# Four edits in a gated mix of a state-space layer and a long convolution: where two steps stand in the head, who scales two tiles, the order of two loads, and how the last tile is finished

## The chip, the cores and the metric

The kernel runs on one core of a Trainium2 chip. A core has five engines that run side by side, each in the order of its own instructions: TensorE (PE in the profile; its weight loads are PEld), VectorE (DVE), ScalarE (ACT), GpSimd (POOL) and SyncE (SP). SP issues loads and stores, POOL issues the transfers that add to their destination. The metric is the time of one execution on the device in microseconds (us).

## The reference, cut to what matters

Two branches of a sequence of 2048 positions with 1024 channels are mixed by a gate that is worked out from x.

```python
g = _sigmoid((x * gate_w).sum(-1, keepdims=True))
a = _A_ref(x, ...)      # a diagonal complex state per p:  h[t] = Lam_bar * h[t-1] + B_bar x[t]
                        # y = 2 Re(h C^T) + x * Dskip
b = _B_ref(x, k, v, ...)  # k: 4 taps per channel; kv = taps(k) * v
                        # y = causal convolution of kv with ssm_k (length 2048), plus kv * ssm_D;  b = x * y
return g * a + (1 - g) * b
```

## The kernel before, in words

**Branch B** (the convolution) runs first, channel block by channel block (eight blocks of 128 channels, index `c`). Taps, foldings and a transform by tables of sines and cosines are matmuls (`taps`, `fold_K`, `fwd_K`, `fwd_V`); the products of the two spectra are made on VectorE (`products`), the way back is matmuls again (`inverse`, tables `CI` and `SI`), and the result goes to a scratch in DRAM (`cv_scr`). ScalarE moves most PSUM tiles to SBUF.

**Branch A** (the state) works on four blocks of 512 positions (`tb`) and four groups of two state tiles (`g`). `Bu` multiplies x by B on TensorE; ScalarE copies the result out of PSUM; `turn_U` scales it on ScalarE into tiles named `Q`, which POOL adds to `U` by transfer; `scan` rotates, runs the recurrence on VectorE and rotates back into `hb`, then makes the odd positions into `U`. `Cy` and `Cy_g` multiply `hb` and `U` by C for each of the 16 output tiles of 128 positions. Every tile of C (eight, `CT[0]` to `CT[7]`) must first be turned (`turn_C`): ScalarE makes a scaled copy `m` of the other half (imaginary against real), the half itself is scaled in place, and the two are added, by POOL's transfer (`by_sum`, tiles 0, 1, 4 and 5) or by VectorE.

**The order** is written out by hand. `put` (line 94 is the line that nearly all instructions show) chains every instruction of an engine behind the one before it, so the order of the Python calls is the order on each engine. Many helpers are generators, and `step` and `run` place their pieces. `filler` (line 1361) takes one piece at a time from the list `on_act` between the pieces of `Bu`.

The places of the four edits:

- The head, lines 1076 to 1120. `angles` is `inverse_angles`, the reduced angles of the inverse table on VectorE; `turns` is `inverse_table` (its Abs, then sine `SI`, then cosine `CI`, all on ScalarE); `sp` is `state_params`, whose second step makes `abv`, the rate `rv` (an exponential on ScalarE) and two more small columns; its third step writes `abv` again, so it waits for `rv`.
- `turn_C`, lines 1274 to 1292, and the main loop over 16 scans, lines 1433 to 1480. Tiles 4 and 5 lend their `m` from the four buffers `Q` that `turn_U` uses too.
- The loads on SP around line 1241: C's tiles 0, 1 and 2, with B's third block `BT[2]` in between; then, at line 1295, B's fourth block `BT[3]` and C's tile 3.
- The last block of four output tiles, lines 1482 to 1500. The four PSUM tiles (two banks each: two halves of 512 channels) take groups 0 to 2 of all four tiles, then group 3 tile by tile. `finish` multiplies the B part by x beforehand, then takes a tile out of PSUM, on VectorE (tiles 0, 2 and 3 of the block) or by ScalarE and one addition (tile 1), and stores it; tile 3 is finished in two halves, and its matmuls of the last tile are sorted so that the first half is done first.

PSUM has room for four such tiles, which are taken in turn; a fifth waits until the first has been read.

Of the kernel before, what the change touches and what calls it, by code (L numbers as in the profile page):

```python
# [9 lines left out]
ALU = mybir.AluOpType  # L10
# [10 lines left out]
def kernel(  # L21
# [37 lines left out]
    NT = S // 128  # L59
# [45 lines left out]
    def tt(o, a, b, op):  # L105
        put("dve", V.tensor_tensor, out=o, in0=a, in1=b, op=op)
# [863 lines left out]
    def rows_of(ap, t_):  # L970
        t0 = t_ // 4 * TB + t_ % 4 // 2 + t_ % 2 * HB
        return ap[t0:t0 + HB - 1:2, :]
# [34 lines left out]
        act(gd, rows_, func=ACT.Identity, scale=gcols[:, t_:t_ + 1])  # L1007
        gather(pbb, gd)

    def Cy_g(tb, tl, ps, g, last):  # L1010
        X = hbs[tb, g] if tl < 2 else Us[tb, g][1]
        tsl = slice(tl % 2 * 128, tl % 2 * 128 + 128)
        steps_ = [(j, c, dh) for j in range(2) for c in range(2) for dh in range(2)]
        if tb * 4 + tl == NT - 1:
            steps_.sort(key=lambda s_: s_[2])
        for j, c, dh in steps_:
            mm(ps[dh], X[:, c, j, tsl], CT[2 * g + j][:, c, dh * 512:(dh + 1) * 512],
               g == 0 and j == 0 and c == 0, last and j == 1 and c == 1)

# [13 lines left out]
    def product(t_):  # L1033
        pbb, xr = ios[t_]
        tt(xr, xr, pbb, ALU.mult)
# [3 lines left out]

    def store(t_):  # L1040
        move(rows_of(of, t_), gas.pop(t_))

    def finish(t_, ps=None):

        rows = rows_of(of, t_)
        product(t_)
        xr = ios.pop(t_)[1]
        if ps is None:
            yield
            ga = gas.pop(t_)  # L1050
            tt(ga, ga, xr, ALU.add)
        else:
            yield
            ga = a_room(t_)
            for o, i in ps:
                put("dve", V.scalar_tensor_tensor, out=ga[:, o], in0=i, scalar=gcols[:, t_:t_ + 1], in1=xr[:, o],
                    op0=ALU.mult, op1=ALU.add)
                if len(ps) > 1:
                    move(rows[:, o], ga[:, o])
            if len(ps) > 1:  # L1060
                return
        move(rows, ga)


    def step(gen):
        next(gen, None)
# [31 lines left out]
    step(sp)  # L1098
    run(first)
    dg1 = dgs(1, True)  # L1100
    run(angles)
    load("kT", 1)
    load("v", 1)
    load("kn", 1)
    fwd_K(0, (0, 1))
    fwd_V(0, (0, 1))
    step(sp)
    step(turns)
    taps(1, dg1)
    step(sp)  # L1110
    step(turns)
    p0 = products(0, 0)
    steps(p0, 3)
    tv = times_v(1)
# [17 lines left out]
    for c in range(NC - 1):  # L1132
        n, nn = c + 1, c + 2
        if c == 0:
            load("kn", 2)
            load("kT", 2)
            load("v", 2)
            load_BT(0, 0)
            load_xT(0, (0,))
            p1 = products(0, 1)  # L1140
            fwd_K(n, (0, 1))
            step(p0)
            run(tv)
            dg = dgs(nn, True)
            steps(p1, 2)
            step(p0)
            step(p1)
            run(p0)
            taps(nn, dg)
            step(sp)  # L1150
            fwd_K(n, (2, 3))
            step(p1)
            step(sp)
            fwd_V(n)
            run(p1)
            run(fold_K(nn))
            tv = times_v(nn)
            step(tv)
            load("kn", 3)
            load("kT", 3)  # L1160
            load_BT(0, 1)
            apart = spread(3)
            step(apart)
            load_xT(0, (1,))
            run(apart)
            lam_diag(0, lam_pool, True)
            continue
        if c == 6:
            put("pool", nc.gpsimd.tensor_copy, stamp, xTs[2][:, 0, 0:HB + 1:HB])
        tabs, back, prod = turn_table(c - 1) if c <= NG else none, inverse(c - 1), products(c)  # L1170
        step(old)
        step(tabs)
        if c == 6:
            step(parts)
        step(back)
        step(tv)
        steps(prod, 3)
        run(tv)
        step(old)
        step(tabs)  # L1180
        run(back)
        run(old)
        fk = none
        if nn < NC:
            dg = dgs(nn)
            if by_channel(nn):
                fk = fold_columns(nn)
                step(fk)
        if c == 2:
            step(parts)  # L1190
        fwd_K(n, (0, 1))
        if c in (2, 6):
            step(parts)
        fwd_K(n, (2, 3))
        if c == 4:
            step(parts)
        if c == 6:
            run(sp)
            s5p["Q"] = s5p["wu"]
            run(turns_U[2])  # L1200
            gate(0)
        step(prod)
        if nn < NC:
            if not by_channel(nn):
                fk = mirror_K(nn)
            step(fk)
            if c < 5:
                step(fk)
            if c == 4:
                step(parts)  # L1210
            if c == 1:
                load_BT(1, 0, True)
            elif c < 5:
                load("v", nn, True)
            step(parts)
            taps(nn, dg)
            if c == 5:
                load("v", nn)
                load_xT(2, held=True)
            if nn + 1 < NC:  # L1220
                load("kT", nn + 1, True)
                load("kn", nn + 1)
                apart = spread(nn + 1)
                step(apart)
                if c == 1:
                    load_BT(1, 1)
                elif c in (2, 3):
                    load_xT(1, (3 - c,))
                run(apart)
        step(prod)  # L1230
        run(fk)
        if n == NC - 1:
            overlap_K(n)
        run(prod)
        if nn < NC:
            tv = times_v(nn)
            step(tv)
            step(parts)
        else:
            run(next(tiles))  # L1240
            for pi in range(3):
                CT[pi] = ld.tile([128, 2, D], BF16, name="CTa", tag="ld")
                if pi == 0:
                    hold(CT[0][:, 0, 0:1])
                load_CT(pi)
                if pi == 0:
                    load_BT(2, 0)
                    load_BT(2, 1)
            run(next(tiles))
            run(next(tiles))  # L1250
        fwd_V(n, (0, 1))
        if c < 6 and c != 4:
            step(parts)
            if c in (1, 3):
                step(parts)
        fwd_V(n, (2, 3))
        if c in (4, 5):
            step(parts)
        if c == 1:
            lam_diag(1, lam_pool)  # L1260
        old = tabs
# [12 lines left out]
    def turn_C(pi):  # L1274
        by_sum = pi in (0, 1, 4, 5)
        if pi in (4, 5):
            m = [s5p["Q"].tile([128, D], BF16, name="Q") for c in range(2)]
        else:
            whole_m = m_pool.tile([128, 2, D], BF16, name="m")
            m = [whole_m[:, c] for c in range(2)]  # L1280
        for c in range(2):
            act(m[c], CT[pi][:, 1 - c], func=ACT.Identity, scale=mc2i[:, pi:pi + 1])
            yield
        for c, f in enumerate((c2r, mc2r)):
            if pi < 2:
                act(CT[pi][:, c], CT[pi][:, c], func=ACT.Identity, scale=f[:, pi:pi + 1])
            else:
                ts(CT[pi][:, c], CT[pi][:, c], f[:, pi:pi + 1], None, ALU.mult)
            if by_sum:
                gather(CT[pi][:, c], m[c])  # L1290
        if not by_sum:
            tt(CT[pi], CT[pi], whole_m, ALU.add)

    turning = [turn_C(pi) for pi in range(NP)]
    load_BT(3, 0)
    load_BT(3, 1)
    load_CT(3)
    with tc.tile_pool(name="fin", bufs=1, side="right") as fin:

# [133 lines left out]
    for j in range(NS):  # L1433
# [6 lines left out]
        advance(j)  # L1440
        for t in turning[2 * j:2 * j + 2]:
            run(t)
        on_act += [lambda t=t: step(t) for t in turning[2 * j + 2:2 * j + 4] for _ in range(2)]
        turn = turns_U[turned[j]] if j in turned else none
        if j != 10 and plan[j][0:1] != "G":
            step(turn)
# [34 lines left out]

    tb = NTB - 1
    t0 = tb * 4
    pss = []
    for tl in range(4):
        ps = ps2([128, 2, 512], "psy")
        halves = [(slice(h * 512, h * 512 + 512), ps[:, h]) for h in range(2)]
        pss.append(([ps[:, 0], ps[:, 1]], halves if tl == 3 else [(slice(0, D), flat(ps))]))
    for g in range(NG - 1):
        for tl in range(4):  # L1490
            Cy_g(tb, tl, pss[tl][0], g, False)
    fins = []
    for tl in range(4):
        fins.append(finish(t0 + tl, None if tl == 1 else pss[tl][1]))
        step(fins[tl])
    for tl in range(4):
        Cy_g(tb, tl, pss[tl][0], NG - 1, True)
        if tl == 1:
            scale_a(t0 + tl, pss[tl][1])
        run(fins[tl])  # L1500
# [1 line left out]
_INS = ['A_x', 'A_Lambda_re', 'A_Lambda_im', 'A_B_re', 'A_B_im', 'A_C_re', 'A_C_im', 'A_log_dt', 'A_Dskip', 'B_q', 'B_k', 'B_v', 'B_shift_k', 'B_ssm_k', 'B_ssm_D', 'gate_w']  # L1502
_OUTS = [((1, 2048, 1024), 'bfloat16')]
# [25 lines left out]
```

## Time and profile before

| | us |
|---|---|
| median of 3 runs | 384.97 (384.64 to 386.58) |
| the profiled execution, its own time | 384.57 |
| its span, first to last instruction | 382.8 |
| TensorE busy | 371.3 |
| VectorE busy | 371.2 |
| ScalarE busy | 303.6 |
| GpSimd busy | 81.8 |
| granted TensorE clock | 0.998 |

A row of the timeline holds start, length, engine, line, operation, what is written and read, the shapes, the count of merged instructions, and in brackets the idle time of the engine before it and what ended it. A row with a count merges neighbours of one kind; its length runs to the last one's end. A row of the chain holds start, length and what the chain went through. A weight load stands in front of every matmul, on its own track, while the matmul before it runs. About one matmul record in fifty is missing.

### The profile page before, as it was taken

The page shows a single profiled execution, that of the slowest core. Times are in us where ns is not written, and L with a number is a line of the kernel's source. Part 1 is how long each engine was busy: PE and PEld are TensorE (multiplying, and loading weights), DVE is VectorE, ACT ScalarE, POOL GpSimd, SP SyncE. Part 2 cuts the span into 40 slices and gives each one's busy share as a digit, 9 for nine tenths or more (in the row PEclk, how much of TensorE's full clock was granted, in tenths as well). Part 3 has the DMA queues.
Part 4 walks back from the last instruction along what each step waited for, and adds up shares of the span by engine and source line. Part 5 has one row for each costly group of instructions (what it writes and reads, how often), then busy time and mean ns, then how long its engine had stood idle before and what let it go on. Part 6 is the DMA issues. An engine that isn't in the chain of part 4 may idle for free.

```text
span 382.8 us, 6633 instructions
## 1 busy us (share of the span) xinstructions
PE 371.3 (97%) x2419; PEld 198.3 (52%) x2453; DVE 371.2 (97%) x599; ACT 303.6 (79%) x469; POOL 81.8 (21%) x108
## 2 busy tenths in 40 slices
PE   7899999999999999999999999989999999999995
PEld 5566458575584846744454444434444444444442
DVE  7999999999999999999999999999999999999996
ACT  5898998988979999786979699675989759937601
POOL 4011030020301102031003110413414323634100
PEclk9999999999999999999999999999999999999999
DMA  7979999998999997959999999986899999898903
GB/s 166 165 108 223 218 205 205 245 203 211 201 164 211 208 213 169 198 125 154 192 221 164 226 203 250 213 153 125 150 222 192 208 245 246 136 250 156 238 8 110
DMA packets 126402, 71.77 MB, mean 187 GB/s; under 512 B 104665, under 2 KB 107489, under 8 KB 126370
## 3 DMA queue, kind: packets, MB, share of 16 engines
q1 hardware_dynamic: 111232, 45.64, 55.4%
q0 software_dynamic: 12976, 25.17, 38.9%
q10 hardware_dynamic: 2162, 0.54, 0.8%
q8 instruction: 19, 0.31, 0.3%
q14 instruction: 13, 0.11, 0.1%
HBM read 15.48 MB, written 8.39 MB: 62 GB/s over the span
## 4 chain that ended last, share of the span: by engine, by line
PE 52%; DVE 30%; issue 9%; DMA 4%; ACT 3%; ACTq 1%; POOL 0%; DVEq 0%; POOLq 0%
PE psy L94 29%; PE both L94 15%; DVE BT L94 11%; DVE wkh L94 8%; DVE G L94 5%; DVE t L94 3%; PE psz L94 2%; DVE ks L94 2%; PE psk L94 2%; DMA CT<-Q 2%; DMA pbb<-cv_scr 1%; PE psv L94 1%; DMA rows<-in_gate_w_dram 1%; PE p L94 1%; PE taps L94 1%
## 5 line engine op out<-in xcount | busy, mean ns | idle before, releaser
L94 PEld LDWEIGHTS <-BT 128*128 128x128 bf16 x640 | 62.0, 98 | 48.3 <-issue 0.2
L94 PE MATMUL both<-xT,BT 128*128 128x512 bf16 x375 | 83.0, 379 | 0.4
L94 POOL DMA_DIRECT2D U<-Q x26 | 26.7, 1039 | 88.8 <-ACT Q L94 31.0
L94 PEld LDWEIGHTS <-hb 128*128 128x128 bf16 x256 | 24.9, 98 | 31.4 <-issue 1.6
L94 PEld LDWEIGHTS <-U 128*128 128x128 bf16 x240 | 23.5, 98 | 28.3
L94 PE MATMUL psy<-CT,hb 128*128 128x512 bf16 x157 | 36.3, 379 | 0.1
L94 ACT ACTIVATE Vh<-psv 128x1024 bf16<-128x1024 f32 x32 | 30.7, 1034 | 5.3 <-PE psv L94 5.3
L94 PE MATMUL psy<-CT,U 128*128 128x512 bf16 x149 | 34.6, 379 | 0.2
L94 ACT ACTIVATE Q<-U,lam 128x512 bf16<-128x512 bf16 (+1 forms) x52 | 29.9, 612 | 4.9 <-DMA CT<-Q 4.9
L94 DVE TENSOR_TENSOR_SCAN W<-rv,init,A 128x256 bf16<-128x256 f32 x48 | 32.2, 730 | 0.0
L94 POOL DMA_DIRECT2D G<-wkh x8 | 9.7, 1218 | 102.8 <-DVE wkh L94 102.8
L94 ACT ACTIVATE U<-both 128x512 bf16<-128x512 f32 x44 | 24.1, 595 | 8.0 <-PE both L94 7.5
L94 PEld LDWEIGHTS <-SF 128*128 128x128 bf16 x184 | 18.0, 98 | 19.7 <-issue 1.4
L94 PE MATMUL psk<-eok,SF 128*128 128x512 bf16 (+1 forms) x119 | 27.9, 354 | 0.3
L94 PE MATMUL psz<-G,CI 128*128 128x512 bf16 x64 | 24.3, 379 | 0.1
L94 PE MATMUL psz<-G,SI 128*128 128x512 bf16 x64 | 24.3, 379 | 0.0
L94 PE MATMUL psy<-CTa,hb 128*128 128x512 bf16 x94 | 22.6, 379 | 1.2 <-ACT U L94 1.0
L94 PE MATMUL taps<-dg,kT 128*128 128x128 bf16 (+1 forms) x352 | 21.7, 210 | 0.8 <-DMA kT<-in_B_k_dram 0.8
L94 PEld LDWEIGHTS <-kT 128*128 128x128 bf16 x352 | 21.0, 100 | 2.5 <-DMA kT<-in_B_k_dram 2.1
L94 DVE TENSOR_TENSOR wkh<-BT,Vh 128x3072 bf16<-128x3072 bf16 (+4 forms) x20 | 21.8, 1110 | 0.0
L94 DVE TENSOR_TENSOR wkh<-Kh,Vh 128x3072 bf16<-128x3072 bf16 (+2 forms) x16 | 21.2, 1348 | 0.0
L94 PE MATMUL psy<-CTa,U 128*128 128x512 bf16 x87 | 20.4, 379 | 0.1
(227 smaller groups left out, 846.1 us busy)
## 6 DMA issues: line engine op xcount, KB each, us to landing
U<-Q POOLq DMA_DIRECT2D x26, 256.0 KB, 5.3
G<-wkh POOLq DMA_DIRECT2D x6, 768.0 KB, 8.8
cv_scr<-cv SPq DMA_DIRECT2D x16, 256.0 KB, 5.7
kn<-in_B_ssm_k_dram SPq DMA_DIRECT2D x5, 512.0 KB, 4.0
v<-in_B_v_dram SPq DMA_DIRECT2D x5, 512.0 KB, 6.2
out_dram<-m SPq DMA_DIRECT2D x8, 256.0 KB, 4.5
BT<-cv_scr SPq DMA_DIRECT2D x7, 256.0 KB, 5.9
out_dram<-BT SPq DMA_DIRECT2D x7, 256.0 KB, 2.0
```

The lines of the kernel that those rows point to most:

```text
L94: i = f(*a, **kw)
```

## The change

1. **Head.** The second step of `state_params` moves up from behind the transforms, to stand between the first and the second tile of `fwd_K` and ahead of the angles; the step of the inverse table that makes the sine moves behind the second half of the first block's spectra, next to the cosine.
2. **C's tiles 4 and 5.** Their scaling in place moves from VectorE to ScalarE (`by_sum` instead of `pi < 2`), as two more pieces of their generators; the list of pieces for ScalarE no longer takes those of tiles 2 and 3, and takes four instead of two of tiles 4 and 5. So tile 4 is turned whole among the pieces of `Bu` 9, and tile 5 among those of `Bu` 10.
3. **Loads.** C's tile 2 is allocated and loaded after `BT[3]`, ahead of C's tile 3.
4. **The last tile.** Its second half gets a PSUM tile of its own, `rest`, and all its 16 matmuls (four groups) come after everything else. Its first half is taken out by ScalarE and one addition (`scaled_added`), the second by VectorE (`added`); the products stand directly ahead of each tile's end instead of all in front.

```diff
-    run(angles)
     load("kT", 1)
     load("v", 1)
     load("kn", 1)
-    fwd_K(0, (0, 1))
+    fwd_K(0, (0,))
+    step(sp)
+    run(angles)
+    fwd_K(0, (1,))
     fwd_V(0, (0, 1))
-    step(sp)
     step(turns)
     taps(1, dg1)
     step(sp)
-    step(turns)
     p0 = products(0, 0)
...
-            for pi in range(3):
+            for pi in range(2):
                 CT[pi] = ld.tile([128, 2, D], BF16, name="CTa", tag="ld")
...
         for c, f in enumerate((c2r, mc2r)):
-            if pi < 2:
+            if by_sum:
                 act(CT[pi][:, c], CT[pi][:, c], func=ACT.Identity, scale=f[:, pi:pi + 1])
             else:
                 ts(CT[pi][:, c], CT[pi][:, c], f[:, pi:pi + 1], None, ALU.mult)
             if by_sum:
                 gather(CT[pi][:, c], m[c])
+                yield
...
     load_BT(3, 0)
     load_BT(3, 1)
+    CT[2] = ld.tile([128, 2, D], BF16, name="CTa", tag="ld")
+    load_CT(2)
     load_CT(3)
...
-        on_act += [lambda t=t: step(t) for t in turning[2 * j + 2:2 * j + 4] for _ in range(2)]
+        if j > 0:
+            on_act += [lambda t=t: step(t) for t in turning[2 * j + 2:2 * j + 4] for _ in range(4 if j == 1 else 2)]
...
+    def added(t_, o, ps):
+        put("dve", V.scalar_tensor_tensor, out=a_room(t_)[:, o], in0=ps, scalar=gcols[:, t_:t_ + 1],
+            in1=ios[t_][1][:, o], op0=ALU.mult, op1=ALU.add)
+        move(rows_of(of, t_)[:, o], a_room(t_)[:, o])
+
+    def scaled_added(t_, o, ps):
+        ga, xr = a_room(t_), ios[t_][1]
+        act(ga[:, o], ps, func=ACT.Identity, scale=gcols[:, t_:t_ + 1])
+        tt(ga[:, o], ga[:, o], xr[:, o], ALU.add)
+        move(rows_of(of, t_)[:, o], ga[:, o])
+
+    pss = [ps2([128, 2, 512], "psy") for tl in range(4)]
+    banks = [[ps[:, 0], ps[:, 1]] for ps in pss]
     for g in range(NG - 1):
         for tl in range(4):
-            Cy_g(tb, tl, pss[tl][0], g, False)
...
+            Cy_g(tb, tl, banks[tl], g, False, (0, 1) if tl < 3 else (0,))
     for tl in range(4):
...
+        Cy_g(tb, tl, banks[tl], NG - 1, True, (0, 1) if tl < 3 else (0,))
+        product(t0 + tl)
+        if tl < 3:
+            (scaled_added if tl == 1 else added)(t0 + tl, slice(0, D), flat(pss[tl]))
+        else:
+            scaled_added(t0 + tl, slice(0, 512), banks[tl][0])
+    rest = ps2([128, 2, 512], "psy")[:, 0]
+    for g in range(NG):
+        Cy_g(tb, 3, [None, rest], g, g == NG - 1, (1,))
+    added(t0 + 3, slice(512, D), rest)
```

`Cy_g` has one more argument, the halves that it multiplies, and the sorting for the last tile is gone. The matmuls are the same 2453 in number.

## The prediction

> **What bounds the kernel now.** I read the page's first part, then the chain in order of time, then the busy times by stretch, then the timelines of the four places that the diff touches.
>
> ```profile
> span 382.8 us, 6633 instructions
> PE 371.3 (97%) x2419; PEld 198.3 (52%) x2453; DVE 371.2 (97%) x599; ACT 303.6 (79%) x469; POOL 81.8 (21%) x108
> ```
>
> ```profile
> 164.30 0.39 PE mirror L94
> ...
> 253.15 9.01 PE psy L94 x41
> ...
> 374.96 3.63 PE psy L94 x16
> ```
>
> ```profile
> 32.00:164.00 132.00, 130.46 (x1107) 82.86 (x1116) 131.41 (x126) 117.06 (x181) 16.63 (x21) 1.00 1.05 206
> 164.00:251.00 87.00, 86.20 (x477) 40.50 (x487) 86.10 (x135) 72.08 (x120) 19.13 (x21) 1.00 1.02 196
> 253.00:378.00 125.00, 124.22 (x595) 56.96 (x607) 122.92 (x274) 87.56 (x135) 39.26 (x46) 1.00 0.85 174
> ```
>
> The columns behind the length are busy PE, PEld, DVE, ACT, POOL, then the granted clock and the DMA share. Two engines are full at once: from 32 to 378 us neither TensorE nor VectorE idles by as much as 2% of a stretch. The chain runs over VectorE before 164, over TensorE after it. So an edit is worth time only if it takes work or a wait from both, or leaves the one that it doesn't help in no one's way. No edit changes TensorE's work; it can gain waits alone, and VectorE gains what is taken from it.
>
> **Head.** VectorE, then ScalarE, then TensorE:
>
> ```profile
> 19.86 0.18 DVE L94 TENSOR_TENSOR abv<-pcol 128x16 f32<-128x16 f32 x1 [1.05 <-ACT rv L94]
> 20.39 1.17 DVE L94 TENSOR_TENSOR G<-BT,Vh 128x2048 bf16<-128x2048 bf16 x1
> 23.48 1.22 DVE L94 TENSOR_TENSOR ks<-ks,v 128x2048 bf16<-128x2048 bf16 x1
> 29.91 0.69 DVE L94 TENSOR_TENSOR ev<-ks,lo 128x1024 bf16<-128x1024 bf16 x1 [0.32 <-PE psv L94]
> ```
>
> ```profile
> 16.88 1.02 ACT L94 ACTIVATE BT<-psk 128x1024 bf16<-128x1024 f32 x1 [0.49 <-PE psk L94]
> 17.80 1.94 ACT L94 ACTIVATE Vh<-psv 128x1024 bf16<-128x1024 f32 x2
> 22.18 1.02 ACT L94 ACTIVATE ks<-taps 128x1024 bf16<-128x1024 f32 x1 [0.50 <-PE taps L94]
> 23.22 1.28 ACT L94 ACT_TABLE_LOAD   x1
> 24.51 1.06 ACT L94 ACTIVATE SI<-BT 128x1024 bf16<-128x1024 f32 x1
> ```
>
> ```profile
> 47.79 0.39 PE L94 MATMUL mirror<-ks,refl 128*128 128x512 bf16 x1 [0.37 <-DVE ks L94]
> ```
>
> The step of the rates goes ahead of the inverse angles on VectorE and of the second spectrum's eviction on ScalarE, where `rv` falls into the 0.49 that ScalarE idles anyway. The 1.05 at 19.86 goes. Not all of it is kept: `G` must wait for the end of `Vh` (17.80 + 1.94 = 19.74), 0.6 ahead of 20.39, and three steps on `ks` waits for ScalarE's second tap tile, 22.18 + 1.02 = 23.20, which TensorE sets. So `ks` starts at 23.23 to 23.25, 0.25 sooner. Then the table load and the inverse sine (23.22 to 25.57, 2.3 us) no longer stand ahead of the next evictions; these run some 1.1 sooner, held by TensorE's own pace, and the wait of 0.32 at 29.91 goes. Together 0.57 for VectorE (bounds: nothing, and both idles, 1.37; 0.57 because the tap tile's end is in a row). The sine and the load are paid later, behind `Vh`, where they push the next evictions back by about 1.4; the tap tiles' wait for TensorE behind them takes that up. If that cover were gone, 1.4 would fall on ScalarE alone. TensorE waits for VectorE at each mirror (47.79, and 164.30 in the chain), so it is 0.57 sooner as well.
>
> **C's tiles 4 and 5 of the code (the fifth and sixth).** ScalarE, VectorE, GpSimd and TensorE, one fence each:
>
> ```profile
> 225.75 1.57 ACT L94 ACTIVATE U<-both 128x512 bf16<-128x512 f32 x3
> 229.16 2.19 ACT L94 ACTIVATE Q<-CT,mc2i 128x1024 bf16<-128x1024 bf16 x2
> 244.49 1.13 ACT L94 ACTIVATE gd<-rows,gcols 128x1024 bf16<-128x1024 bf16 x1
> 250.54 1.34 ACT L94 ACTIVATE Q<-U,lam 128x512 bf16<-128x512 bf16 x2 [4.92 <-DMA CT<-Q]
> 252.01 2.06 ACT L94 ACTIVATE U<-both 128x512 bf16<-128x512 f32 x4
> ```
>
> ```profile
> 243.96 0.48 DVE L94 TENSOR_SCALAR CT<-CT,c2r 128x1024 bf16<-128x1024 bf16 x1
> ...
> 245.55 0.68 DVE L94 TENSOR_TENSOR trn<-TCS,U 128x1024 bf16<-128x1024 bf16 x1
> ```
>
> ```profile
> 244.74 3.63 POOL L94 DMA_DIRECT2D CT<-Q  x4 [6.62 <-DVE CT L94]
> ```
>
> ```profile
> 217.41 34.70 PE L94 MATMUL both<-xT,BT 128*128 128x512 bf16 x156
> 253.15 2.75 PE L94 MATMUL psy<-CTa,hb 128*128 128x512 bf16 x12 [1.04 <-ACT U L94]
> ```
>
> VectorE loses four scalings: 245.55 − 243.96 = 1.59. ScalarE gets them at half of 2.19 less the overlap, 1.04 each: 4.16, into its idle of 4.92, which goes because the gathers leave as each half is scaled, around 231 to 239. It reaches the evictions of 252.01 some 0.8 sooner (4.92 − 4.16), and up to 0.3 more from short waits it no longer meets; TensorE's 1.04 at 253.15 falls to about 0.1. I take 1.0. On the way ScalarE evicts B's tiles up to 4.2 late. A tile takes 16 matmuls of 0.216 (34.70 over 156 and the missing records, ten tiles) = 3.46, and four PSUM tiles come round in turn. From 225.75 on ScalarE has, up to the end of B11's first tile, ten scalings at 1.04, ten evictions at 0.49 and four small copies at 0.2: 242.0. TensorE wants that PSUM tile back eight tiles after 217.41, at 245.0: 3.0 of cover. GpSimd issues the four gathers ahead of both `pbb` gathers instead of between them; the first of these leaves some 4 later, for a product that VectorE does only after C's last tiles are turned, well behind 245.55.
>
> **B's last block ahead of C's third tile.** On SP two loads change places. TensorE shows no wait in 164 to 251 (86.20 of 87, the rest missing records), so the block's sooner arrival gains nothing, and C's third tile is turned just ahead of the row at 225.75, behind the block's matmuls, which end before 217.41. I cost it at nothing; if that distance were gone, the price is a load's landing:
>
> ```profile
> CT<-in_A_C_re_dram SPq DMA_TRANSPOSE x5, 4.8
> ```
>
> **Tail.** VectorE and the weight loads:
>
> ```profile
> 370.74 0.49 DVE L94 TENSOR_TENSOR hb<-hb,trn 128x256 bf16<-128x256 bf16 x2
> ...
> 372.67 2.49 DVE L94 TENSOR_TENSOR xlast<-xlast,BT 128x1024 bf16<-128x1024 bf16 x4
> 375.08 1.27 DVE L94 SCALAR_TENSOR_TENSOR BT<-psy,gcols,xlast 128x1024 bf16<-128x1024 f32 x1
> ...
> 378.62 1.41 DVE L94 SCALAR_TENSOR_TENSOR BT<-psy,gcols,xlast 128x512 bf16<-128x512 f32 x2 [0.42 <-PE psy L94]
> ```
>
> ```profile
> 371.30 3.33 PEld L94 LDWEIGHTS <-hb 128*128 128x128 bf16 x16
> ```
>
> Twelve matmuls (three groups by four, the last tile's second half) leave the place ahead of the last group: it comes 12 × 0.216 = 2.59 sooner. Its second index is the fifth load, 371.30 + 4 × 0.216 = 372.16; VectorE has its first half at 370.74 + 0.29 = 371.03. That slack of 1.13 is all there is. With TensorE 1.57 and VectorE 0.57 + 1.59 = 2.16 sooner, TensorE waits 2.59 + 1.57 − 1.13 − 2.16 = 0.87. So VectorE sets the end: TensorE's last matmul moves by 2.59 − 1.13 − 2.16 = −0.70. Behind it now stand two steps of VectorE, 1.41 together, both held by the last matmul; afterwards one of 0.75: −0.66. The cover for the other tiles: from the last `hb` VectorE has 1.44 (371.23 to 372.67), four products of 0.62, two steps of 1.24 and two sums of about 0.6 and 0.35: 7.4; TensorE has 40 matmuls, 8.8. So they end some 1.4 ahead; without that the last step would queue. The fifth PSUM tile waits for tile 12's step, done 3.4 behind `hb`, and is wanted 24 matmuls behind it, 5.2.
>
> **Sum.** −2.16 + 2.59 − 1.13 − 0.66 = −1.36 against the profiled execution: span 382.8 to 381.4, its time 384.57 to 383.21. The median of the runs, 384.97, is 0.40 above that execution, so 383.6.
>
> **Rivals.**
> (1) VectorE keeps both idles of the head, 1.37: then 2.96, and −2.96 + 0.80 = −2.16: 382.8. Against it stands the tap tile's row. If VectorE came early enough that TensorE set the end, −1.57 − 0.66 = −2.2: 382.7.
> (2) The head gives nothing, since `ks` and TensorE hold it: 1.59 alone, −0.79: 384.2.
> (3) On the other side: VectorE is stopped at one product.
>
> ```profile
> 330.42 2.87 POOL L94 DMA_DIRECT2D row<-gd  x1
> ```
>
> ```profile
> row<-gd POOLq DMA_DIRECT2D x1, 256.0 KB, 11.5
> ```
>
> ```profile
> 342.40 0.66 DVE L94 TENSOR_TENSOR row<-row 128x1024 bf16<-128x1024 bf16 x1
> ```
>
> That gather lands at 330.42 + 11.5 = 341.9, only 0.5 ahead of its product. GpSimd's queue runs from landing to landing there. If it moves with VectorE, nothing happens: it starts from a scaling that waits for VectorE,
>
> ```profile
> 266.68 2.56 ACT L94 ACTIVATE q<-hb,lam 128x512 bf16<-128x512 bf16 x4 [2.49 <-DVE hb L94]
> ```
>
> and I take that. If its landings stay where they are, VectorE keeps 0.50 of 2.16, and the sum is +0.30: 385.3. Landings 1.6 later than now make it slower by 0.5% (386.9); each us costs one. TensorE's wait in front of the last group would then be 2.5 to 4.1.
>
> The Trainium skill, "TensorE: Matmul & The Clock Gate", Part 1, says that the clock falls to half after an idle window of about 3.4 us. The trace agrees as far as it goes: the clock stays at 1.00 in all three stretches, and the one wait of 1.04 lies between two of them; no run here shows a longer wait. By the page the far end of this rival would pay about 1.7 more (an estimate: one such window at half rate), near 388.6; the forecast's 0.87 stays under it.
>
> (4) ScalarE's 4.16 stop TensorE for PSUM: only past the 3.0 of cover, each us beyond costing one. Nothing speaks for it but the tightness.
>
> **How the numbers follow.** 0.5%, 1.9 us, is about what a measurement tells from no change: 383.05 and 386.9 are the marks. The forecast has 0.52, its own range 382.8 to 384.4 (terms of 0.3 in the head, 0.3 in the tail, the runs' spread); a quarter of that lies below 383.05. Rival 1 has 0.20, nearly all below it; rival 2 0.14, within; rivals 3 and 4 0.14, half of it above 386.9. Faster 0.33, within 0.59, slower 0.08. For the range I leave out 1 in 10 on each side: 382.4 to 385.3.
>
> **What would show it.** Head: no idle before the second `abv`, `ks` at 23.2, the mirror of 47.79 at 47.2. C: no ScalarE idle of 4.9 near 245 and TensorE's wait before C's first tile under 0.3. Tail: a TensorE wait of about 0.9 on `hb` in the last group, then 40 matmuls without a gap and one VectorE step. I am wrong if VectorE idles anywhere between 30 and 370, if that wait is missing, or if it is above 2.

## The result, and the profile after

The changed kernel takes 383.19 us in the median of 7 runs (382.93 to 384.01); the kernel before, measured beside it, 384.64. The ratio is 0.996, with a 95% interval of 0.9941 to 0.9979: a gain of 1.45 us, clear of no change, and 0.4% where the prediction drew its mark at 0.5%. Measured again later, the changed kernel came to 383.09 against 384.81, ratio 0.9948 (0.9929 to 0.9967). The forecast was 383.6, within 382.4 to 385.3, most likely within 0.5%. Slow runs, which lie over 1.5% above the fastest of their kernel (two of the kernel before, two of the last kernel below), are left out of all medians, ranges and ratios.

The first part of the page of the changed kernel, as above of before:

```profile
span 382.2 us, 6666 instructions
PE 373.0 (98%) x2453; PEld 198.3 (52%) x2453; DVE 369.9 (97%) x595; ACT 308.6 (81%) x474; POOL 80.6 (21%) x108
```

VectorE has lost 1.3 of work (371.2 to 369.9), ScalarE has gained 5. The profiled execution (384.01) is the slowest of the seven, and its span is only 0.6 shorter than before's. The timelines of VectorE tell most of the reason. Its first `ev` step stands ahead of every edit. First the kernel before, then the changed one:

```profile
13.25 1.22 DVE L94 TENSOR_TENSOR ev<-ks,mirror 128x1024 bf16<-128x1024 bf16 x1 [0.41 <-PE foldk L94]
```

```profile
13.82 1.22 DVE L94 TENSOR_TENSOR ev<-ks,mirror 128x1024 bf16<-128x1024 bf16 x1 [0.41 <-PE mirror L94]
19.24 0.17 DVE L94 TENSOR_TENSOR abv<-pcol 128x16 f32<-128x16 f32 x1
20.11 1.23 DVE L94 TENSOR_TENSOR G<-BT,Vh 128x2048 bf16<-128x2048 bf16 x1 [0.24 <-ACT Vh L94]
23.58 1.23 DVE L94 TENSOR_TENSOR ks<-ks,v 128x2048 bf16<-128x2048 bf16 x1 [0.24 <-ACT ks L94]
31.58 1.22 DVE L94 TENSOR_TENSOR G<-BT,Vh 128x2048 bf16<-128x2048 bf16 x1
...
369.51 0.49 DVE L94 TENSOR_TENSOR hb<-hb,trn 128x256 bf16<-128x256 bf16 x2
...
378.70 0.75 DVE L94 SCALAR_TENSOR_TENSOR BT<-psy,gcols,xlast 128x512 bf16<-128x512 f32 x1 [0.66 <-PE psy L94]
```

This execution starts 0.57 late, because its first loads landed later: the first step of VectorE that needs `kn` starts at 10.12 instead of 9.54, after a wait for its load in both. So distances are measured from that `ev` below. The 1.05 in front of the second `abv` is gone; `G` and `ks` wait 0.24 each where the prediction had put them. TensorE of the changed kernel:

```profile
47.37 0.60 PE L94 MATMUL mirror<-ks,refl 128*128 128x512 bf16 x2 [0.37 <-DVE ks L94]
60.19 0.23 PE L94 MATMUL taps<-dg,kT 128*128 128x64 bf16 x2 [0.62 <-DMA kT<-kT]
164.22 0.60 PE L94 MATMUL mirror<-ks,refl 128*128 128x512 bf16 x2 [0.37 <-DVE ks L94]
251.96 1.24 PE L94 MATMUL psy<-CTa,hb 128*128 128x512 bf16 x5
...
369.86 2.76 PE L94 MATMUL psy<-CT,hb 128*128 128x512 bf16 x12 [1.10 <-DVE hb L94]
```

Counted from the first `ev`, it is 0.99 ahead at the mirror of 47.79 (33.55 instead of 34.54); then it waits 0.62 for a transfer that the prediction did not speak of (the last copy of the fourth block's `kT`), and at the mirror of 164.30 it is 0.65 ahead (150.40 instead of 151.05). The wait of 1.04 ahead of C's first tile is gone. The new wait on `hb` is there, 1.10. The chain then runs over TensorE alone, and one VectorE step follows:

```profile
369.86 8.82 PE psy L94 x40
```

### The profile page after: what moved, and what is told of

The parts are those of the page before. It is cut to its first block, busy times and chain, and to the rows that moved or that the text cites. A ratio compares the mean times of both kernels' runs of the same rounds, so it can differ in the third digit from the quotient of the medians.

```text
span 382.2 us, 6666 instructions
## 1 busy us (share of the span) xinstructions
PE 373.0 (98%) x2453; PEld 198.3 (52%) x2453; DVE 369.9 (97%) x595; ACT 308.6 (81%) x474; POOL 80.6 (21%) x108
## 4 chain that ended last, share of the span: by engine, by line
DVE 38%; PE 32%; ACT 11%; DMA 10%; issue 7%; ACTq 1%; POOL 1%; SPq 0%; DVEq 0%; POOLq 0%
DVE W L94 7%; PE psk L94 7%; PE both L94 5%; DVE BT L94 4%; DVE hb L94 4%; PE psv L94 4%; DVE trn L94 4%; DVE A L94 4%; DVE U L94 3%; PE taps L94 3%; DVE wkh L94 3%; ACT Q L94 3%; DMA CTa<-m 2%; DVE q L94 2%; PE psy L94 2%
```

## The experiments

Every execution starts a little differently, so this table holds, for VectorE in each profiled execution, the start of the first `ev`, of the last two sums of `hb` and the end of the last step, with the two distances, TensorE's wait on `hb` in the last group, and the medians of the runs, of the kernel and of before beside it.

| kernel | first `ev` | last `hb` | end | ev to hb | hb to end | wait on hb | median | before |
|---|---|---|---|---|---|---|---|---|
| before | 13.25 | 370.74 | 380.03 | 357.49 | 9.29 | none | 384.64 | |
| changed | 13.82 | 369.51 | 379.45 | 355.69 | 9.94 | 1.10 | 383.19 | 384.64 |
| changed, again | 13.02 | 368.51 | 378.46 | 355.49 | 9.95 | 1.21 | 383.09 | 384.81 |
| head alone | 13.32 | 374.41 | 383.88 | 361.09 | 9.47 | none | 385.18 | 385.10 |
| C's tiles alone | 13.18 | 368.94 | 380.63 | 355.76 | 11.69 | none | 385.07 | 385.10 |
| tail alone | 14.03 | 371.61 | 381.56 | 357.58 | 9.95 | 0.94 | 385.40 | 385.10 |
| loads alone | 13.21 | 370.60 | 380.13 | 357.39 | 9.53 | none | 384.74 | 385.10 |
| head undone | 13.18 | 368.95 | 378.90 | 355.77 | 9.95 | 0.77 | 383.60 | 384.63 |
| C's tiles undone | 13.15 | 370.31 | 380.25 | 357.16 | 9.94 | 1.36 | 384.73 | 384.63 |
| tail undone | 13.81 | 369.42 | 378.74 | 355.61 | 9.32 | none | 383.19 | 384.63 |
| first index first | 13.58 | 369.19 | 378.39 | 355.61 | 9.20 | none | 382.80 | 384.81 |
| k first | 12.89 | 368.12 | 378.06 | 355.23 | 9.94 | 1.04 | 383.09 | 384.81 |
| products on GpSimd | 13.14 | 377.27 | 385.70 | 364.13 | 8.43 | 6.49 (first index) | 390.36 | 384.81 |
| best guess | 14.06 | 369.84 | 378.43 | 355.78 | 8.59 | none | 382.57 | 384.63 |

Ahead of the first edit the kernels do the same, yet `ev` starts at 12.89 to 14.06; and with the head of before, the `G` of 32.00 lies 18.52 to 18.77 behind `ev` in five profiles. So differences of 0.2 between two profiles say little.

**Theory:** VectorE sets the end through `hb`; the head and C's tiles bring `hb` sooner, the new tail lengthens what lies behind it. **Rivals:** TensorE sets the end and the tail is free; or the head gives nothing because a transfer holds TensorE.

### Each edit alone on the kernel before

**Head alone.** The edit is the first hunk of the diff above.

> Before, with the edit of the head alone. Theory of the prediction: VectorE keeps 0.57 of its idles and TensorE follows at every mirror, so the time falls by 0.57 (ratio 0.9985), the mirror of 47.79 comes at 47.2 and the one of 164.30 at 163.7. Rival, from the trace of the changed kernel: from the end of ks (24.70 before) SP issues its transposed loads one behind the other, and the third copy of the fourth block's k, which TensorE reads at 59.7, comes from that chain; then TensorE can keep no more ahead of 60 than ks does (0.25 or less), it waits up to 0.6 at its taps near 60, and the mirror of 164.30 comes 0.1 to 0.3 sooner: ratio 0.9993 or nearer to 1. Second rival: nothing is gained at all, and the mirror of 47.79 stays.

Measured: 385.18 (383.93 to 388.56) against 385.10, ratio 1.000 (0.9966 to 1.0034). The profiled execution was its slowest, 388.56, and shows two things: TensorE and its clock, then VectorE.

```profile
46.95 0.39 PE L94 MATMUL mirror<-ks,refl 128*128 128x512 bf16 x1 [0.37 <-DVE ks L94]
...
153.03 0.22 PE L94 MATMUL taps<-dg,kT 128*128 128x64 bf16 x2 [2.23 <-DMA kT<-kT]
```

```profile
153.00:157.00 4.00, 3.97 (x69) 3.85 (x70) 3.96 (x6) 1.51 (x2) 0.00 (x0) 0.57 0.70 127
```

```profile
31.17 1.22 DVE L94 TENSOR_TENSOR G<-BT,Vh 128x2048 bf16<-128x2048 bf16 x1
...
263.58 0.69 DVE L94 TENSOR_TENSOR xr<-xr,pbb 128x1024 bf16<-128x1024 bf16 x1 [3.21 <-DMA pbb<-gd]
```

The mechanism works: `G` of 32.00 starts 17.85 behind the first `ev` (18.75 before), the mirror of 47.79 comes at 46.95. That is more than the 0.57 expected. But then a copy of the last block's `kT` lands late, TensorE waits 2.23 and runs at a clock of 0.57 in the mean of the next 4 us, and later VectorE waits 3.21 for a `pbb` gather. This execution cannot give the edit's worth at the end, and the runs spread too far to show it; the run with the head undone, below, comes closer to it.

**C's tiles alone**, with the list of pieces.

> Before, with the scaling of C's tiles 4 and 5 on ScalarE and the new list of pieces alone. Theory of the prediction: VectorE saves 1.59, TensorE its wait of 1.04 ahead of C's first tile, and since TensorE has the later end in before's tail (its weights wait 1.13 less than they could) the time falls by 1.0 (ratio 0.9974). Rival: ScalarE's four scalings stop TensorE for PSUM near 245, each us past the cover of 3.0 costs one, and the gain is under 0.3 (ratio above 0.999).

Measured: 385.07 against 385.10, ratio 0.9986 (0.9958 to 1.0014), and a wait of TensorE that neither theory held:

```profile
203.58 6.65 PE L94 MATMUL both<-xT,BT 128*128 128x512 bf16 x29 [1.79 <-DMA BT<-in_A_B_im_dram]
```

It waits for B's last block. The weight load and the landing time of that block in the kernel before, and the landing here:

```profile
201.66 0.10 PEld L94 LDWEIGHTS <-BT 128*128 128x128 bf16 x1
...
196.97 1.72 SPq L94 DMA_TRANSPOSE BT<-in_A_B_im_dram  x1
...
BT<-in_A_B_im_dram SPq DMA_TRANSPOSE x1, 4.6
```

```profile
BT<-in_A_B_im_dram SPq DMA_TRANSPOSE x1, 6.3
```

In the kernel before the block lands at 196.97 + 4.6 = 201.57, and the weight load that needs it starts at 201.66: a slack of 0.1, which looks like no wait at all. Here it took 6.3. VectorE has its 1.6 (ev to hb 355.76, 1.73 less than before, of which 0.16 was there ahead of the edit), TensorE sets the end, and the wait eats its gain. In this execution C's tiles are worth nothing at the end without the third edit. Whether the other runs met the same wait is not known; their median shows no gain either.

**Tail alone.**

> Before, with the new last tile alone. Theory of the prediction: the last group comes 2.59 sooner, only 1.13 of which is slack, so TensorE waits for the second index of hb by about 1.5, its last matmul comes 1.1 sooner less what of the 2.59 is lost, that is 1.13 of wait less: last matmul 2.59 - 1.46 = 1.13 later by the same 12 matmuls behind the wait, that is +1.46, one VectorE step fewer behind it -0.66: the time rises by 0.80 (ratio 1.0021). Rival: TensorE sets the end and the 12 moved matmuls cost nothing, only the step behind the last matmul goes: -0.66 (ratio 0.9983), and no wait on hb is seen.

Measured: 385.40 against 385.10, ratio 1.0004 (0.9979 to 1.0030). Times do not tell, the profile does: from the first `ev` to the end it is 367.53 against 366.78, 0.75 longer, where the sum of the theory was 0.80. VectorE is where it was (ev to hb 357.58 against 357.49), the wait on `hb` is 0.94, and the end lies 9.95 behind `hb` instead of 9.29: 0.66 of the 0.75 is the tail's. In this profile the tail by itself costs, and the rival (free, and no wait) falls. The wait was expected at 1.46, and is smaller because TensorE reached the last group later in this execution, which also waited 1.58 for a copy of `ks` at 157.85; with VectorE setting the end that does not matter.

**Loads alone.**

> Before, with B's last block loaded ahead of C's third tile alone. Theory of the prediction: nothing moves (ratio 1.000, TensorE without a wait from 164 to 251 as before, VectorE without an idle). Rival: C's third tile lands later than its scaling wants it near 225, ScalarE or VectorE waits there for a load by up to 4.8 (its landing time), and the time rises by up to that (ratio up to 1.012).

Measured: 384.74 against 385.10, ratio 0.9984 (0.9963 to 1.0005): no change clear of its interval, and no wait at 201. TensorE waited 1.92 at the same copy of the last block's `kT` as above (there 2.23), VectorE was not held up by it (ev to hb 357.39), and the clock stayed:

```profile
153.36 0.22 PE L94 MATMUL taps<-dg,kT 128*128 128x64 bf16 x2 [1.92 <-DMA kT<-kT]
```

```profile
153.00:157.00 4.00, 3.64 (x80) 3.50 (x81) 3.96 (x6) 2.14 (x4) 0.07 (x1) 1.00 0.91 188
```

### The changed kernel again, and with one edit undone

**A second execution in profile.**

> The changed kernel once more, for a second execution in profile. Theory: the head is worth 0.8 to VectorE (0.84 in the run of the head alone), and what the first profile of the changed kernel shows less at the tail is a late transfer, the third copy of the fourth block's k, for which TensorE waited 0.62 at 60.19; where that copy is in time, VectorE has the second index of hb 2.2 to 2.5 sooner than before (370.74), at 368.3 to 368.6, and the span is 381.2 to 381.4. Rival: the lead is lost in every execution, the wait near 60 and the 369.5 come back.

TensorE's rows, then VectorE's:

```profile
46.65 0.60 PE L94 MATMUL mirror<-ks,refl 128*128 128x512 bf16 x2 [0.37 <-DVE ks L94]
...
163.14 0.60 PE L94 MATMUL mirror<-ks,refl 128*128 128x512 bf16 x2 [0.37 <-DVE ks L94]
...
368.86 2.76 PE L94 MATMUL psy<-CT,hb 128*128 128x512 bf16 x12 [1.21 <-DVE hb L94]
```

```profile
211.07 0.69 DVE L94 TENSOR_TENSOR A<-TCS,U 128x1024 bf16<-128x1024 bf16 x1
...
335.69 1.29 DVE L94 TENSOR_TENSOR xtwo<-xtwo 128x1024 bf16<-128x1024 bf16 x2 [0.29 <-issue]
...
368.51 0.49 DVE L94 TENSOR_TENSOR hb<-hb,trn 128x256 bf16<-128x256 bf16 x2
...
377.71 0.75 DVE L94 SCALAR_TENSOR_TENSOR BT<-psy,gcols,xlast 128x512 bf16<-128x512 f32 x1 [0.66 <-PE psy L94]
```

No wait near 60, a lead of 1.16 still there at 163.14 (0.23 of it the earlier start), `hb` at 368.51 and a span of 381.2: the numbers of the theory came. Its reason, the late copy, is the smaller part. Of the 1.00 by which `hb` comes sooner than in the first profile, 0.80 is the start (first `ev` at 13.02 instead of 13.82), and 0.20 is left. What the late copy cost the first profile is 0.28 at the mirror of 164.30 (150.40 behind `ev` there, 150.12 here). A wait of 0.28 to 0.77 near 60 stands in five of the nine profiles with the head's edit and in none of the five without it (one of the five rows names ScalarE instead of the copy), so it seems to be met where TensorE comes sooner.

One loss is common to both: VectorE idles 0.28 to 0.29 in front of `xtwo`. An idle of 0.28 to 0.31 stands there in all seven profiles that have both the head and C's edit, and in none with one of them undone. Six of the profiles name nothing that it waits for, the last kernel's names a landing of `Q` in `U`; why it comes was not found.

**Head undone.**

> The changed kernel with the head's edit taken back. Theory: VectorE and TensorE both come 0.8 to 0.9 later from 33 us on (G behind the third eviction of Vh at 32.0 again, the mirror of the fourth block 0.8 later), VectorE sets the end through hb, so the end comes 0.8 to 0.9 later: ratio to the changed kernel 1.0022. By the prediction's term it would be 0.57. Rival: nothing is lost, since a load near 60 holds TensorE in either case.

Measured: 383.60 (383.23 to 384.03) against 383.09 and 383.19 with it: 0.4 to 0.5. These were not measured beside each other; the ratio to before is 0.9973 (0.9961 to 0.9985), and its interval overlaps those of the changed kernel. Its `G`, two later steps of VectorE, its mirror and its wait on `hb`:

```profile
31.70 1.23 DVE L94 TENSOR_TENSOR G<-BT,Vh 128x2048 bf16<-128x2048 bf16 x1
...
211.94 0.69 DVE L94 TENSOR_TENSOR A<-TCS,U 128x1024 bf16<-128x1024 bf16 x1
...
336.11 1.29 DVE L94 TENSOR_TENSOR xtwo<-xtwo 128x1024 bf16<-128x1024 bf16 x2
```

```profile
47.49 0.60 PE L94 MATMUL mirror<-ks,refl 128*128 128x512 bf16 x2 [0.37 <-DVE ks L94]
...
369.30 2.76 PE L94 MATMUL psy<-CT,hb 128*128 128x512 bf16 x12 [0.77 <-DVE hb L94]
```

From the first `ev` to `G` it is 18.52 here, 17.76 and 17.84 with the edit: 0.7 at that place. Over all profiles it is 18.64 in the mean without the edit and 17.84 with it: 0.8.

VectorE's instructions behind branch B are the same in both kernels, so the lead can be followed. Against the second execution it is 0.71 at the first step of branch A (211.94 - 13.18 against 211.07 - 13.02) and 0.26 at `xtwo`, where this kernel has no idle; at `hb` it is 0.28 (355.77 to 355.49). Against the first execution, which met the late copy, it is 0.43 and 0.08 at these places, and 0.08 at `hb`. So in both 0.35 is lost at `xtwo`, most of it the idle of 0.28; the second execution loses another 0.10 on the way, near 303. The 0.8 to 0.9 expected did not reach the end: 0.1 to 0.3 of it did in the profiles, and the 0.4 to 0.5 of the medians is not clear of the noise.

**C's tiles undone.**

> The changed kernel with the scaling of C's tiles 4 and 5 back on VectorE and the old list of pieces. Theory: the second index of hb comes 1.6 later, TensorE meets its wait of about 1.04 ahead of C's first tile again, waits for hb in the last group by 1.6 - 1.0 more than the 1.1 to 1.2 of the changed kernel, and the end lies 9.95 behind that hb as before: 1.6 later, ratio to the changed kernel 1.0042. Rival: VectorE's four steps fall into slack, and only TensorE's 1.0 is lost.

```profile
252.50 1.67 PE L94 MATMUL psy<-CTa,hb 128*128 128x512 bf16 x7 [0.98 <-ACT U L94]
...
370.66 2.76 PE L94 MATMUL psy<-CT,hb 128*128 128x512 bf16 x12 [1.36 <-DVE hb L94]
```

384.73 against 383.09 and 383.19, 1.5 to 1.6 as expected; TensorE's wait ahead of C's first tile is back with 0.98, and the end lies 9.94 behind `hb`. The ratio to before is 1.001 (0.9990 to 1.0029): without this edit nothing of the gain is left. It carries the result.

**Tail undone.**

> The changed kernel with the last tile as before. Theory: without the 12 matmuls moved behind the last group TensorE meets no wait on hb; its lead of 2.1 over before (0.9 from the head, 1.1 from C's wait) holds to its last matmul, and two steps of VectorE stand behind it, 1.41 and 0.42 of waiting: the end comes 2.0 sooner than before's, that is 0.6 to 0.7 sooner than the changed kernel's: span 380.5 to 380.8, ratio to the changed kernel 0.9982. So the new tail costs where it was forecast to gain nothing more. Rival: the old tail's two steps behind the last matmul and VectorE's order cost as much as the wait, and the time is that of the changed kernel or longer by up to 0.66.

Its last rows on VectorE:

```profile
369.42 0.49 DVE L94 TENSOR_TENSOR hb<-hb,trn 128x256 bf16<-128x256 bf16 x2
...
377.33 1.41 DVE L94 SCALAR_TENSOR_TENSOR BT<-psy,gcols,xlast 128x512 bf16<-128x512 f32 x2 [0.42 <-PE psy L94]
```

In the profile the old tail is better by 0.6: no wait on `hb`, the end 9.32 behind it instead of 9.95, and from the first `ev` to the end 364.93 against 365.44 and 365.63. The times do not confirm it: 383.19 (382.34 to 384.58), the same as the changed kernel, with a wider spread. Its profiled execution started as late as the changed kernel's first (13.81), so the span of 381.5 misses the 380.5 to 380.8 expected. What can be said: no gain from the new tail shows, and in the profiles it cost 0.5 to 0.7.

The changed kernel with the old order of the loads was not run, so what that edit is worth beside the others is not shown.

### Four versions past the changed kernel

**First index first**: the last group's two indices are split.

```diff
     for tl in range(4):
-        Cy_g(tb, tl, banks[tl], NG - 1, True, (0, 1) if tl < 3 else (0,))
+        Cy_g(tb, tl, banks[tl], NG - 1, True, (0, 1) if tl < 3 else (0,), (0,))
+    for tl in range(4):
+        Cy_g(tb, tl, banks[tl], NG - 1, True, (0, 1) if tl < 3 else (0,), (1,))
         product(t0 + tl)
```

> The changed kernel, with the first index of all four tiles of the last group ahead of the second index of any. It tells what sets the end. Theory: TensorE's wait on hb goes (1.10 in the changed kernel), its last matmul comes some 1.1 sooner, but VectorE's steps behind the last hb, 8.5 of work, then stand without a gap, so the end comes only by VectorE's last wait sooner: 0.66, that is 9.3 behind the start of the last two sums of hb instead of 9.94. Rival: TensorE alone sets the end, and it comes 1.1 sooner. Second rival: nothing, for the fifth PSUM tile makes TensorE wait instead.

```profile
369.19 0.49 DVE L94 TENSOR_TENSOR hb<-hb,trn 128x256 bf16<-128x256 bf16 x2
...
377.30 0.42 DVE L94 TENSOR_TENSOR BT<-BT,xlast 128x512 bf16<-128x512 bf16 x1
377.64 0.75 DVE L94 SCALAR_TENSOR_TENSOR BT<-psy,gcols,xlast 128x512 bf16<-128x512 f32 x1
```

The wait on `hb` is gone, and VectorE runs from `hb` to the end without one: 9.20 instead of 9.94, 0.74 against the 0.66 expected, and not the 1.1 that TensorE won. This is the test of what sets the end, and VectorE it is. The median is 382.80 (382.51 to 383.23), ratio to before 0.994 (0.9917 to 0.9963), the lowest ratio here; its interval overlaps that of the changed kernel.

**K first**: `load("kT", 3)` ahead of `load("kn", 3)`.

> The changed kernel, with the fourth block's k loaded ahead of its ssm_k, so that its copies leave 0.6 sooner. Theory: TensorE has no wait for the copy of kT near 60, and the lead of VectorE that the head gives is still there at the mirror of 164.3, at 163.4 to 163.7; the time falls by 0.2 to 0.4 against the changed kernel (ratio to before 0.995). Rival: the copy's landing does not depend on when its chain starts, the wait near 60 is seen again, or ssm_k comes late at 55.4 and TensorE waits there.

Measured 383.09 (382.64 to 387.54), ratio 0.9966 (0.9941 to 0.9991): the 0.2 to 0.4 expected against the changed kernel do not show. Its mirror of 164.30 comes at 162.92, 150.03 behind the first `ev`, and its profile has no wait near 60; but the second execution of the changed kernel had none either (150.12), and the last kernel below has one of 0.31 with the same order. Not settled.

**Products on GpSimd**, on top of first index first:

```diff
+        if by_pool:
+            put("pool", nc.gpsimd.tensor_tensor, out=xr, in0=xr, in1=pbb, op=ALU.mult)
```

In the order of the program the four products stand ahead of the last block's matmuls.

> As first_index_first, and the four products of the last tiles on GpSimd instead of VectorE. Theory: VectorE's 4 x 0.62 behind the last hb go, TensorE sets the end again, and the last step starts when its last matmul ends: 0.8 to 1.2 sooner than with the first index first alone, that is 8.2 to 8.5 behind the start of the last two sums of hb. Rival: GpSimd's products run beside VectorE's last scans and slow them, so that hb itself comes later by 0.5 to 2 and the gain is gone.

It took 390.36, ratio 1.0148 (1.0115 to 1.0181). GpSimd, VectorE, TensorE and its clock:

```profile
356.79 8.66 POOL L94 TENSOR_TENSOR xlast<-xlast,BT 128x1024 bf16<-128x1024 bf16 x4
```

```profile
356.57 9.44 DVE L94 TENSOR_TENSOR hb<-TCS,W 128x1024 bf16<-128x1024 bf16 x1
```

```profile
367.34 5.48 PE L94 MATMUL psy<-CT,hb 128*128 128x512 bf16 x16 [6.49 <-DVE hb L94]
```

```profile
367.00:369.00 2.00, 1.66 (x4) 0.58 (x5) 1.97 (x6) 1.29 (x3) 0.00 (x0) 0.50 0.01 4
```

The rival came, and larger: one VectorE step stood 9.44 (0.69 in the changed kernel) until GpSimd's four products were done. Behind the second index of `hb` the end lay 8.43 away, inside the 8.2 to 8.5 of the theory, and the last step waited 1.31 for TensorE, as it said. But TensorE had first waited 6.49 and run at half clock here, so where it stood against `hb` was another, and the agreement can be chance.

**Best guess**: first index first, k first, and all tiles but the last half taken out by ScalarE (`scaled_added` in place of `added`).

> The changed kernel with the first index of all four tiles ahead of the second, tiles 0 and 2 of the last block taken out by ScalarE and one addition as tile 1 is, and the fourth block's k loaded ahead of its ssm_k. Theory: VectorE's two steps of 1.24 become two of 0.61, so its work behind the last hb ends ahead of TensorE's last matmul, which then sets the end, 0.4 to 0.5 sooner than with the first index first alone; the end lies 8.8 to 8.9 behind the last two sums of hb (9.2 there, 9.95 in the changed kernel), and span is 380.0 to 380.3 where the loads are in time. Rival: ScalarE's three evictions of 1.12 come one behind the other and the fifth PSUM tile or the last sum waits for them: then 9.2 or more.

```profile
373.14 0.69 DVE L94 TENSOR_TENSOR BT<-BT,xlast 128x1024 bf16<-128x1024 bf16 x1 [0.69 <-ACT BT L94]
...
377.68 0.75 DVE L94 SCALAR_TENSOR_TENSOR BT<-psy,gcols,xlast 128x512 bf16<-128x512 f32 x1
```

The end lies 8.59 behind `hb`, better than the 8.8 to 8.9 expected, and 364.37 behind the first `ev` (365.44 in the changed kernel). The mechanism is not the one expected: the last step does not wait for TensorE, so VectorE still sets the end, after 0.69 of waiting for ScalarE's first eviction. The median of seven runs is 382.57 (381.58 to 385.27), ratio 0.9951 (0.9927 to 0.9976). The interval overlaps that of the changed kernel, so the gain in the profile is not shown in the times.

## Why the prediction was right or wrong

- **The bound** was read rightly: with both engines full, VectorE's last `hb` sets the end, the wait of TensorE in front of it was forecast at 0.87 and came to 1.10 and 1.21, and one VectorE step stands behind the last matmul.
- **The sum**, -1.36, holds from the first `ev` on: -1.15 in the first profile (365.63 against 366.78), -1.34 in the second; the medians say -1.45 and -1.72. The terms behind it are less right than their sum, and it is in part luck that they cancel: VectorE's 2.16 came to 1.80 and 2.00 at `hb`, and the tail's cost of 0.80 to 0.65. Of the 0.41 by which the median lies under the forecast, 0.33 is that before's median, of three runs then, fell from 384.97 to 384.64.
- **Head**, 0.57: mis-sized twice. At `G` of 32.00 it is worth 0.8, since `ks` came 0.47 sooner and not 0.25 (9.76 behind the first `ev` instead of 23.48 - 13.25 = 10.23); the tap tile that it waits for, taken as fixed, had moved up too. At `hb` 0.1 to 0.3 is left. Two steps failed. "TensorE waits for VectorE at each mirror, so it is 0.57 sooner as well": between two mirrors a copy of `kT` can land late for a TensorE that comes sooner, and in the first profile that took 0.28 from the lead. And the lead was taken to last to the end: 0.35 of it is lost at `xtwo`.
- **C's tiles**: 1.59 and 1.0 are confirmed (1.57 at `hb` when alone, 1.5 to 1.6 in the times and a wait of 0.98 back when undone). The evictions that run late stopped TensorE nowhere, so rival 4 did not come. The 4.92 of ScalarE's idle are gone: `Q<-U,lam` follows `gd` at 249.36 without a wait.
- **Loads, "I cost it at nothing"**: wrong as reasoned. "TensorE shows no wait in 164 to 251" was taken for slack; it was 0.1. In two of the other three kernels profiled with the old order TensorE waited there (1.79 and 0.18), in none with the new order. That the edit guards the other gains rather than adding one of its own is argued from these waits, not shown.
- **Tail**: alone it cost 0.66 behind `hb`, where its own arithmetic has 0.80. VectorE's work behind the last `hb` took 8.05 (370.00 to 378.05 in the first profile) and not 7.4, so the cover ahead of its last step was 0.66 and not 1.4; it was enough. But the prediction's numbers already held that without it the change would be worth -1.57 rather than -1.36, and it did not say so; the traces say 0.5 to 0.7 lost, the times nothing.
- **"I am wrong if VectorE idles anywhere between 30 and 370"**: by this sign the prediction was wrong, by the 0.28 in front of `xtwo`; the other two signs (the wait missing, or above 2) did not come.
- **Rivals 1 and 2**: the head did not keep 1.37. That it gives nothing at the end (rival 2) is not excluded, though not for the reason given: `ks` and TensorE did not hold it at `G`. **Rival 3** did not come at `row`; that the mechanism exists shows in the run of the head alone, where VectorE lost 3.21 to another gather.

## What to carry to other kernels

A wait that is not in the profile is not slack: read the landing time of the transfer against the start of what needs it, and take 0.1 us as a wait that other executions will have. Where two engines are full, measure each edit from a step ahead of all edits to the step that sets the end, since executions differ by more at their start than the edit is worth. Work moved behind the last dependency of the bounding engine can cost, even if it fills the other engine better: here 0.5 to 0.7 in the profiles, though the medians do not show it. A lead won early has to be followed to the end, step by step, against a kernel without the edit.

## What the runs showed of the hardware

- GpSimd's products of two operands stopped VectorE outright: a step of 0.69 took 9.44 while four of them ran for 8.66. The Trainium skill, "SBUF — State Buffer", section "Who interferes with whom", calls the port pair that the two share an exclusive lock. This case agrees; and the VectorE step, though its row starts 0.22 sooner, was kept waiting through all four.
- The granted clock was 0.57 in the mean of the 4 us behind a TensorE wait of 2.23, 1.00 behind one of 1.92, and 0.50 behind one of 6.49. The Trainium skill, "TensorE: Matmul & The Clock Gate", Part 1, sets the idle window at about 3.4 us. The 6.49 agrees with it; the 2.23 shows that here a shorter wait was enough, and the measurement decides. One run each gives no threshold.
- TensorE met the same copy of the last block's `kT` in time in twelve of fourteen profiles and waited 1.92 and 2.23 for it in two, whose edits (the loads, the head) stand far from it.
